# Key maxima behind a given step's minima, decode spread over steps 1 to 7, later attention loads on ScalarE's queue

## The chip, the core and the metric

The kernel runs on one core of one Trainium2 chip. The metric is device microseconds of one execution. Engines are TensorE (PE, with PEld its weight loads), VectorE (DVE), ScalarE (ACT), GpSimd (POOL) and SyncE (SP); "q" behind an engine's name is its instruction sequencer, which also issues DMAs.

## What is computed

Block-local attention over 2 batches, 8 heads, 768 positions and 64 channels, then two blocks of matrix products on its output.

```python
k_sum = k.reshape(B, H, nb, block, D).max(axis=3)      # nb = 24 blocks of 32 keys
v_sum = v.reshape(B, H, nb, block, D).mean(axis=3)
scores_l = scale * q @ k^T, only where |i - j| < 16
scores_s = scale * q @ k_sum^T + log(32)
a = softmax(concat([scores_l, scores_s]))
x = a @ concat([v, v_sum])                             # (2, 768, 512)
u = x + (relu(x^T @ w_tok1) @ w_tok2)^T ; x = u + relu(u @ w_ch1) @ w_ch2
out = x + relu(layernorm(x) * g @ moe2_w_ch1) @ moe2_w_ch2
```

## The kernel before

Attention works on 8 pairs of heads (i = 0 to 7), each in 3 steps, so there are 24 steps (n = 0 to 23, pair n // 3). A step covers four windows of 64 queries. Its parts are: `att_qk`, sixteen small score matmuls against 96 local keys and 24 block maxima; `att_exp`, on VectorE four fused instructions that scale, mask and take the minima of a window (the "minima"), and on ScalarE four exponentials; `att_tr`, transposes on TensorE; `att_evac`, ScalarE's copy out of PSUM; `att_av`, the product with the values; `att_norm`, VectorE's division; `att_hi` and `att_lo`, the split of the result for later products.

Before its first step each pair needs its loads (`load_pair`: keys, 480 KB, and queries, 384 KB; `load_v`: two value transfers of 306 KB; `load_vt`: transposed values, pairs 4 to 7), the maxima of its key blocks (`prep_k`, one VectorE reduction, and `copy_k` on ScalarE), and the sums of its value blocks: by summing matmuls for pairs 0 to 3 (`sum_v`, three parts of eight, and `write_sums` on ScalarE), on GpSimd for pairs 4 to 7 (`prep_v1`).

The scores of two successive steps lie in the same PSUM banks, so the scores of step n + 1 start only when the minima of step n are taken. The key, query and value buffers are three deep and are freed by pair i - 3.

The weights come as 62 "halves" of 128x512, at 64 bits an element. `load_half` loads one into one of three stage buffers. The conversion runs in ticks: a tick takes the magnitude of one half on ScalarE (L114), decodes the half before it by four VectorE instructions (L128, L130, L132, L136), casts an older one on ScalarE (L176), subtracts the cast on VectorE (L183), and issues the next load. A tick counts as four operations for `convert_all(n)` and `convert(n)`, the first tick as one. Only three slots for two halves each exist during attention, so only six halves are cast there; more can be decoded.

`attention` gives every part a due time in units of steps, from the table `ORDER` (L34), and writes the program in the order of due times (L613). TensorE keeps that order exactly. On the other engines and queues a scheduler orders the instructions by its own simulated readiness, with the written order as priority; each engine and queue then runs in order on the chip. Before step 8.58 two filler matmuls follow each step's scores (`fill`). From step 8.58 on the first products on attention's output are laid between the steps (`g1`, `g2`, `transpose_u`). In `before` the attribute `ops` sets how many conversion operations each `att_norm` carries along: none up to due time 3.5, then 3, then 2 from 8.58 on.

Of the kernel before, what the change touches and what calls it, by code (L numbers as in the profile page):

```python
# [14 lines left out]
ALU = mybir.AluOpType  # L15
AX = mybir.AxisListType
# [4 lines left out]
BLOCK, WINDOW = 32, 16  # L21
NB = S // BLOCK
# [4 lines left out]
NK = 96 + NB  # L27
# [4 lines left out]
LEAD = 3  # L32
NXN = 3
ORDER = {  # L34
    "load_k": -5.2, "load_vt": -5.1, "load_v": -4.7, "kmax": -1.3, "copy_k": -1.0, "vsum": -2.4,
    "vput": -0.2, "vsum0": 0.6, "vput0": 1.12, "exp": 0.5, "tr": 1.1, "evac": 1.55, "av": 2.15,
    "norm": 2.6, "hi": 2.65, "lo": 2.7, "conv": 3.5, "bg": 8.58, "fin": 0.97,
}
# [14 lines left out]
class Kern:  # L53
# [150 lines left out]
    def load_pair(self, i, queue=None):  # L204
        nc = self.nc
        queue = queue or nc.sync
        b, p = divmod(i, NPAIR)
        Q, K = self.Q[i % 3], self.K[i % 3]
        nc.sync.dma_start(K[:, 0:6, NB : NB + 160], self.k[b, p])
        queue.dma_start(Q, self.q[b, p])  # L210

    def load_vt(self, i):
        b, p = divmod(i, NPAIR)
        self.nc.sync.dma_start(self.VT[i % 2], self.vt[b, p])

    def load_v(self, i):
        nc = self.nc
        b, p = divmod(i, NPAIR)
        V = self.V[i % 3]
        nc.sync.dma_start(V[NB:NK, 0], self.v[b, p, 0])  # L220
        nc.sync.dma_start(V[0:96, 1], self.v[b, p, 1])

    def prep_k(self, i):
        nc = self.nc
        K = self.K[i % 3]
        ks = self.att.tile([P, NB], F32, tag="ks", bufs=2, name=f"ks{i}")
        nc.vector.tensor_reduce(
            ks.rearrange("p (v j) -> p v j", v=6),
            K[:, 0:6, NB + 16 : NB + 144].rearrange("p v (j k) -> p v j k", k=BLOCK),
            axis=AX.X,  # L230
            op=ALU.max,
        )
        self.ks[i] = ks

    def copy_k(self, i):
# [72 lines left out]
    def att_exp(self, n):  # L308
        nc = self.nc
        qd = n % 3  # L310
        ps = self.sc.pop(n)
        sn = self.att.tile([P, 4, NK], F32, tag="sn", bufs=2, name=f"sn{n}")
        mn = self.att.tile([P, 4], F32, tag="mn", bufs=3, name=f"mn{n}")
        pr = self.att.tile([P, 4, NK], F32, tag="pr", bufs=3, name=f"pr{n}")
        self.pr[n] = pr
        for u in range(4):
            w = 4 * qd + u
            mv = w % 2 if 0 < w < NW - 1 else 2 + w % 2
            nc.vector.tensor_tensor_reduce(  # L319
                sn[:, u],  # L320
                ps[:, u % 2, u // 2, :NK],
                self.mask[:, mv],
                scale=-SCALE,
                scalar=3e38,
                op0=ALU.add,
                op1=ALU.min,
                accum_out=mn[:, u : u + 1],
            )
            nc.scalar.activation(pr[:, u], sn[:, u], AF.Exp, bias=mn[:, u : u + 1], scale=-1.0)  # L329
# [233 lines left out]
    def attention(self):  # L563


        npair, nq = B * NPAIR, 3 * B * NPAIR
        O = ORDER
        ev = []
        put = lambda at, *fns: ev.append((at, len(ev), fns))
        for i in range(npair):  # L570
            at = 3 * i
            if i > 1:
                put(at + O["load_k"], lambda i=i: self.load_pair(i))
                if i >= NPAIR:
                    put(at + O["load_vt"], lambda i=i: self.load_vt(i))
                put(at + O["load_v"], lambda i=i: self.load_v(i))
            put(at + (O["kmax"] if i != 1 else -0.45), lambda i=i: self.prep_k(i))
            put(at + (O["copy_k"] if i != 1 else -0.44), lambda i=i: self.copy_k(i))
            if i < NPAIR:
                for part in range(3):  # L580
                    put((1.15 + 0.5 * part, at + part - 0.75, at + part - 0.75, 7.5 + 0.5 * part)[i], lambda i=i, part=part: self.sum_v(i, part))
                continue
            put(at + O["vsum"], lambda i=i: self.prep_v1(i))
            put(at + O["vput"], lambda i=i: self.prep_v2(i))
        for n in range(nq):
            put(n, lambda n=n: self.att_qk(n))
            if n < O["bg"]:
                put(n + 0.02, lambda: self.fill(2))
            put(n + O["exp"], lambda n=n: self.att_exp(n))
            put(n + O["tr"], lambda n=n: self.att_tr(n))  # L590
            put(n + O["evac"], lambda n=n: self.att_evac(n))
            put(n + O["av"], lambda n=n: self.att_av(n))
            put(n + O["norm"], lambda n=n: self.weave(self.att_norm(n), self.convert(self.ops)))
            put(n + O["hi"], lambda n=n: self.att_hi(n))
            put(n + O["lo"], lambda n=n: self.att_lo(n))
        put(0.0, lambda: self.load_half(0), lambda: self.load_half(1))
        put(O["conv"], lambda: setattr(self, "ops", 3))
        put(O["bg"], lambda: setattr(self, "ops", 2))
        x0, x1, w0, w1 = self.g1(0, 0), self.g1(0, 1), self.g1(1, 0), self.g1(1, 1)
        y, z0 = self.g2(0), self.transpose_u(0)  # L600
        pieces = [x0, x0, x1, x1, y, y, y, y, w0, w0, z0, z0, z0, y, z0, w1, w1, y]
        low = {x0: 5 + O["lo"], x1: 11 + O["lo"], w0: 17 + O["lo"], w1: 23 + O["lo"]}
        need = {x0: 3, x1: 3, w0: 3, y: 6}
        at = O["bg"]
        for k, g in enumerate(pieces):
            while at < low.get(g, 0):
                at += 1
            if g in need:
                put(at, lambda g=g: self.convert_until(need[g]))
            put(at, lambda g=g: self.begin(g))  # L610
            put(at + O["fin"], lambda g=g: self.end(g))
            at += 1
        for _, _, fns in sorted(ev, key=lambda e: e[:2]):  # L613
            for fn in fns:
                fn()
        while self.evacs:
            self.end(self.evacs[0])
# [21 lines left out]
    def run(self):  # L639
        tc, nc, ctx = self.tc, self.nc, self.ctx  # L640
# [11 lines left out]
        self.conv = self.conversion()  # L652
        self.evacs, self.ks, self.ready_xt = [], {}, set()
        self.xt, self.pr, self.pt, self.av, self.sc, self.pst = {}, {}, {}, {}, {}, {}
        self.acc, self.stats, self.xn = {}, {}, {}
        self.add_slots(slots_a, 3)

# [41 lines left out]
        for t in self.V:  # L699
            nc.scalar.dma_start(t[NK : NK + 1], self.guard)  # L700
        nc.sync.dma_start(self.gt, self.g)
        self.load_v(1)

        self.wps = self.ps_mm.tile([P, 512], F32, tag="mm", name="warm_ps")
        self.fill(15)
# [163 lines left out]
```

## Time and profile before

| | us |
|---|---|
| median of three runs | 611.26 (608.82 to 611.40) |
| the profiled execution's own time | 610.87 |
| its span, first to last instruction | 609.1 |
| TensorE busy | 589.4 |
| VectorE busy | 334.0 |
| ScalarE busy | 210.6 |
| mean granted TensorE clock | 0.986 |

Step 23's products with the values end near 107.3 us; what follows is matrix products on attention's output. The difference between the span and the execution's own time, 1.8 us, lies around the program. A share of busy time is a mean over the whole span; a stretch is read by its own rows.

### The profile page before, as it was taken

To read this page: it belongs to the slowest core of one execution; us is meant where nothing else is said; L and a number is where in the kernel's file an instruction comes from. 1 tells how busy PE (TensorE), PEld (TensorE's weight loads), DVE (VectorE), ACT (ScalarE), POOL (GpSimd) and SP (SyncE) were. 2 spreads that over 40 slices of the span, in tenths; PEclk is the share of its full clock that TensorE was granted. 3 is DMA by queue.
4 is the path that set the end of the run, shared out by engine and by line. 5 is a ranking of instruction groups with operands and counts; after the bars stand their busy time and mean duration, and the time that the engine had idled before them with its cause. 6 is when DMAs were issued, how large, how long until landed. Compare 5 with 4: busy or idle time off the path is not lost.

```text
span 609.1 us, 9241 instructions
## 1 busy us (share of the span) xinstructions
PE 589.4 (97%) x3661; PEld 517.0 (85%) x3661; DVE 334.0 (55%) x845; ACT 210.6 (35%) x450; POOL 35.2 (6%) x60
## 2 busy tenths in 40 slices
PE   5889899999999999999999999999999999999997
PEld 2768677879899889899888989999888989989996
DVE  2799765999368799788789951111153211111122
ACT  2697887544133344333444411110122111011110
POOL 2055312100000000000000000000000000000000
PEclk9798899999999999999999999999999999999999
DMA  9977810235224333233423200000000100000011
GB/s 269 317 243 244 255 58 4 70 108 179 93 70 139 103 104 107 101 108 135 135 74 104 70 1 1 0 1 1 0 30 23 53 1 0 1 1 0 1 52 53
DMA packets 21074, 50.40 MB, mean 83 GB/s; under 512 B 1955, under 2 KB 8483, under 8 KB 21030
## 3 DMA queue, kind: packets, MB, share of 16 engines
q1 hardware_dynamic: 20880, 49.39, 24.7%
q8 instruction: 29, 0.48, 0.3%
q10 hardware_dynamic: 150, 0.41, 0.2%
q14 instruction: 15, 0.12, 0.1%
HBM read 46.65 MB, written 3.15 MB: 82 GB/s over the span
## 4 chain that ended last, share of the span: by engine, by line
PE 88%; DMA 4%; ACT 3%; DVE 3%; issue 0%; SPq 0%; POOL 0%; DVEq 0%
PE g L199 2%; PE g L201 2%; PE g L200 2%; PE av L356 1%; ACT pr L329 1%; DMA stage<-in_wts_dram 1%; PE scores L299 1%; DMA V<-in_v_dram 1%; PE pt L336 1%; PE vsum L278 1%; PE tx L517 1%; DMA VT<-in_vt_dram 1%; DMA K<-in_k_dram 1%; ACT V L262 1%; PE tu L450 1%; PE acc_('x', 0)_0_3721 L200 1%
## 5 line engine op out<-in xcount | busy, mean ns | idle before, releaser
L114 ACT ACTIVATE dec<-stage 128x512 f32<-128x512 f32 x62 | 41.9, 675 | 8.1 <-DMA stage<-in_wts_dram 8.1
L136 DVE SCALAR_TENSOR_TENSOR dec<-stage,dec 128x512 uint32<-128x512 uint32 x62 | 43.6, 704 | 0.9
L132 DVE SCALAR_TENSOR_TENSOR dec<-stage,dec 128x512 uint32<-128x512 uint32 x62 | 43.3, 699 | 0.9
L176 ACT CAST wh<-dec 128x512 fp32r<-128x512 f32 x62 | 38.1, 616 | 13.6 <-DVE dec L136 13.4
L183 DVE TENSOR_TENSOR wl<-dec,wh 128x512 fp32r<-128x512 f32 x62 | 42.7, 690 | 0.0
L329 ACT ACTIVATE pr<-sn,mn 128x120 f32<-128x120 f32 x96 | 30.2, 384 | 8.9 <-DVE mn L319 8.8
L128 DVE TENSOR_SCALAR dec<-dec 128x512 f32<-128x512 f32 x62 | 27.1, 440 | 2.5 <-ACT dec L114 2.5
L130 DVE TENSOR_SCALAR dec<-dec 128x512 uint32<-128x512 uint32 x62 | 26.6, 429 | 0.9
L299 PE MATMUL scores<-K,Q 64*64 64x120 f32 x384 | 17.0, 298 | 7.8 <-DVE mn L319 7.2
L319 DVE CUSTOM_DVE_ANT_0 sn<-scores,mask 128x120 f32<-128x120 f32 x96 | 21.3, 277 | 2.5 <-PE scores L299 2.1
L396 POOL TENSOR_TENSOR xl<-u,xh 128x256 fp32r<-128x256 f32 x24 | 18.4, 766 | 66.7 <-ACT xh L387 62.4
L299 PEld LDWEIGHTS scores<-K,Q 64*64 64x64 f32 x384 | 11.1, 146 | 12.7 <-DVE mn L319 7.9
L356 PEld LDWEIGHTS av<-V,PT 121*64 121x64 f32 x384 | 14.2, 143 | 7.3 <-issue 3.6
L356 PE MATMUL av<-V,PT 121*64 121x65 f32 x384 | 17.8, 234 | 2.5 <-ACT V L262 1.9
L278 PE MATMUL vsum<-V,ind 120*120 120x128 f32 (+1 forms) x96 | 15.5, 318 | 1.8 <-ACT V L262 1.8
L336 PE MATMUL pt<-ident,pr 128*120 128x128 f32 x96 | 16.7, 299 | 0.0
L336 PEld LDWEIGHTS pt<-ident,pr 128*120 128x120 f32 x96 | 11.7, 147 | 4.9 <-issue 2.1
L278 PEld LDWEIGHTS vsum<-V,ind 120*120 120x120 f32 (+1 forms) x96 | 13.8, 218 | 2.4 <-ACT V L262 2.0
L199 PE MATMUL g<-xh,wh 128*128 128x256 f32 x48 | 14.1, 293 | 0.5 <-DVE u L433 0.5
L343 ACT COPY PT<-pt 120x512 f32<-120x512 f32 x24 | 13.8, 576 | 1.0 <-PE pt L336 0.8
L492 DVE TENSOR_SCALAR xn<-u,mv,rs 128x128 f32<-128x128 f32 x48 | 14.0, 340 | 0.0
L201 PE MATMUL g<-xh,wl 128*128 128x256 f32 x48 | 13.4, 278 | 0.0
(3003 smaller groups left out, 1695.7 us busy)
## 6 DMA issues: line engine op xcount, KB each, us to landing
stage<-in_wts_dram SPq DMA_DIRECT2D x62, 512.0 KB, 3.3
V<-in_v_dram SPq DMA_DIRECT2D x16, 306.0 KB, 5.0
K<-in_k_dram SPq DMA_DIRECT2D x8, 480.0 KB, 5.9
out_dram<-u SPq DMA_DIRECT2D x12, 256.0 KB, 2.1
Q<-in_q_dram SPq DMA_DIRECT2D x7, 384.0 KB, 5.8
VT<-in_vt_dram SPq DMA_DIRECT2D x4, 384.0 KB, 5.3
Q<-in_q_dram ACTq DMA_DIRECT2D x1, 384.0 KB, 3.1
mask<-in_mask_dram SPq DMA_DIRECT2D x1, 240.0 KB, 5.8
```

What stands on the lines that cost most here:

```text
L114: nc.scalar.activation(m, self.raw[n][:, :, 1].bitcast(F32), AF.Abs)
L128: nc.vector.tensor_scalar(m, m, MAG_LO, MAG_HI, op0=ALU.max, op1=ALU.min)
L130: nc.vector.tensor_scalar(mi, mi, 3, 0x3FFFFFF8, op0=ALU.logical_shift_left, op1=ALU.bitwise_and)
L132: nc.vector.scalar_tensor_tensor(mi, t[:, :, 1], 0xC0000000, mi, op0=ALU.bitwise_and, op1=ALU.bitwise_or)
L136: nc.vector.scalar_tensor_tensor(mi, t[:, :, 0], 29, mi, op0=ALU.logical_shift_right, op1=ALU.bitwise_or)
L176: self.nc.scalar.copy(self.slots[c if c < 16 else c - 16][0][:, s], x)
L183: self.nc.vector.tensor_tensor(wl[:, s], x, f32(wh[:, s]), op=ALU.subtract)
L278: self.nc.tensor.matmul(self.ps_sum[:NK, 0:P].rearrange("p (r c) -> p r c", r=2), self.ind[rows, j, NB - 4 * w : NB - 4 * w + NK], V[rows, ...
L299: nc.tensor.matmul(ps[cols, j, e, :NK], Q[rows, 64 * w : 64 * w + 64], K.rearrange("p v c -> p (v c)")[rows, a : a + NK], start=True, stop ...
L329: nc.scalar.activation(pr[:, u], sn[:, u], AF.Exp, bias=mn[:, u : u + 1], scale=-1.0)
L336: nc.tensor.transpose(ps[:NK, u * P : u * P + P], pr[:, u], self.ident)
L356: nc.tensor.matmul(ps[64 * j : 64 * j + 64, e, 65 * r : 65 * r + 65], pt[:, u * P + 64 * (r ^ j) : u * P + 64 * (r ^ j) + 64], V[:, j, 2 * ...
```

## The change

1. `prep_k`: from pair 1 on the key reduction gets an ordering edge behind the last of the minima of step 3i - 2. The edge is between instructions of VectorE alone.
2. Conversion: `ops` stays 0 until 8.58, and instead two operations are put at n + 0.55 and two at n + 0.8 for n = 1 to 7. The first two weight loads leave the due-time list and are issued in `run`, half 0 ahead of pair 1's values and half 1 behind them.
3. Loads: for pairs 2 to 7 keys, queries, transposed values and values are issued by ScalarE's queue. The values' due time goes from -4.7 to -3.9, relative to the pair's first step.

```diff
-    "load_k": -5.2, "load_vt": -5.1, "load_v": -4.7, ...
+    "load_k": -5.2, "load_vt": -5.1, "load_v": -3.9, ...
 def load_pair(self, i, queue=None):
-        nc.sync.dma_start(K[:, 0:6, NB : NB + 160], self.k[b, p])
+        (nc.sync if i < 2 else queue).dma_start(K[:, 0:6, NB : NB + 160], self.k[b, p])
         queue.dma_start(Q, self.q[b, p])
 def load_vt(self, i):
-        self.nc.sync.dma_start(self.VT[i % 2], self.vt[b, p])
+        (self.nc.sync if i < 2 else self.nc.scalar).dma_start(self.VT[i % 2], self.vt[b, p])
 def load_v(self, i):
-        nc.sync.dma_start(V[NB:NK, 0], self.v[b, p, 0])
-        nc.sync.dma_start(V[0:96, 1], self.v[b, p, 1])
+        queue = nc.sync if i < 2 else nc.scalar
+        queue.dma_start(V[NB:NK, 0], self.v[b, p, 0])
+        queue.dma_start(V[0:96, 1], self.v[b, p, 1])
 def prep_k(self, i):
-        nc.vector.tensor_reduce(ks..., op=ALU.max)
+        with self.tc.issue_after(self.ttr[3 * i - 2].ins) if i > 0 else ExitStack():
+            nc.vector.tensor_reduce(ks..., op=ALU.max)
 def att_exp(self, n):
-            nc.vector.tensor_tensor_reduce(
+            self.ttr[n] = nc.vector.tensor_tensor_reduce(
 def attention(self):
-                put(at + O["load_k"], lambda i=i: self.load_pair(i))
+                put(at + O["load_k"], lambda i=i: self.load_pair(i, self.nc.scalar))
-            put(at + (O["kmax"] if i != 1 else -0.45), lambda i=i: self.prep_k(i))
+            put(at + (O["kmax"] if i != 1 else -0.46), lambda i=i: self.prep_k(i))
             put(n + O["exp"], lambda n=n: self.att_exp(n))
+            if 1 <= n < 8:
+                put(n + 0.55, lambda: self.convert_all(2))
+                put(n + 0.8, lambda: self.convert_all(2))
-        put(0.0, lambda: self.load_half(0), lambda: self.load_half(1))
-        put(O["conv"], lambda: setattr(self, "ops", 3))
 def run(self):
         nc.sync.dma_start(self.gt, self.g)
+        self.load_half(0)
         self.load_v(1)
+        self.load_half(1)
```

## Rows read from the trace of the kernel before

**Rows 1.** Busy time by stretch: us, each engine's busy us (instructions), clock, DMA.
```profile
8.50:26.09 17.59, 10.32 (x93) 8.56 (x92) 10.06 (x38) 9.62 (x24) 0.00 (x0) 0.81 1.07 321
13.87:19.70 5.83, 5.83 (x38) 4.93 (x38) 2.69 (x12) 3.25 (x10) 0.00 (x0) 0.54 1.04 343
26.09:49.21 23.12, 21.27 (x248) 16.66 (x247) 20.99 (x75) 19.50 (x47) 11.55 (x18) 0.87 0.78 249
49.21:70.12 20.91, 18.77 (x265) 15.09 (x264) 18.78 (x77) 16.19 (x41) 10.17 (x15) 0.90 0.79 260
62.63:70.12 7.49, 7.20 (x110) 5.30 (x110) 6.22 (x34) 7.07 (x20) 2.34 (x5) 0.77 1.01 339
70.12:102.49 32.37, 32.29 (x430) 25.75 (x427) 18.83 (x102) 25.72 (x69) 7.42 (x12) 1.00 0.24 69
```

**Rows 2.** TensorE's timeline: start, us, what, [idle before, releaser].
```profile
7.33 0.64 PE L299 MATMUL scores<-K,Q 64*64 64x120 f32 x16 [0.57 <-ACT K L237]
...
13.87 1.07 PE L299 MATMUL scores<-K,Q 64*64 64x120 f32 x16 [5.37 <-DVE mn L319]
...
16.56 3.22 PE L278 MATMUL vsum<-V,ind 120*120 120x128 f32 x16
...
21.16 1.05 PE L278 MATMUL vsum<-V,ind 120*120 120x128 f32 x8
...
26.09 1.08 PE L299 MATMUL scores<-K,Q 64*64 64x120 f32 x16
...
49.21 0.98 PE L299 MATMUL scores<-K,Q 64*64 64x120 f32 x16
...
62.63 0.64 PE L299 MATMUL scores<-K,Q 64*64 64x120 f32 x16 [1.86 <-DVE mn L319]
```

**Rows 3.** VectorE's timeline, the same columns.
```profile
12.06 0.95 DVE L227 TENSOR_REDUCE ks<-K 128x24 f32<-128x768 f32 x1 [5.15 <-DMA K<-in_k_dram]
12.93 0.27 DVE L319 CUSTOM_DVE_ANT_0 sn<-scores,mask 128x120 f32<-128x120 f32 x1
...
21.26 0.27 DVE L319 CUSTOM_DVE_ANT_0 sn<-scores,mask 128x120 f32<-128x120 f32 x1
```

**Rows 4.** ScalarE's timeline, the same columns.
```profile
17.11 0.67 ACT L114 ACTIVATE dec<-stage 128x512 f32<-128x512 f32 x1 [2.58 <-DMA stage<-in_wts_dram]
```

**Rows 5.** The decode's tile up to 110 us: ns min/median/max, first and last start.
```profile
L114 ACT ACTIVATE dec<-stage x10: 650/674/693, 17.1 to 58.4; 128x512 f32<-128x512 f32 x10
L128 DVE TENSOR_SCALAR dec<-dec x10: 415/426/1236, 17.8 to 59.8; 128x512 f32<-128x512 f32 x10
L130 DVE TENSOR_SCALAR dec<-dec x10: 392/422/828, 18.3 to 62.6; 128x512 uint32<-128x512 uint32 x10
L132 DVE SCALAR_TENSOR_TENSOR dec<-stage,dec x10: 675/682/1441, 18.7 to 63.2; 128x512 uint32<-128x512 uint32 x10
L136 DVE SCALAR_TENSOR_TENSOR dec<-stage,dec x10: 660/692/1210, 19.5 to 65.2; 128x512 uint32<-128x512 uint32 x10
...
L183 DVE TENSOR_TENSOR wl<-dec,wh x7: 678/684/878, 22.4 to 109.7; 128x512 fp32r<-128x512 f32 x7
```

**Rows 6.** Stretch 26.09:49.21, line L136 alone: us, busy us (instructions).
```profile
26.09:49.21 23.12, 3.49 (x4) 0.87 0.78 249
```

**Rows 7.** SyncE's queue, 50 to 64 us: start, us that the issue took.
```profile
50.25 0.55 SPq L209 DMA_DIRECT2D K<-in_k_dram  x1
50.85 0.63 SPq L210 DMA_DIRECT2D Q<-in_q_dram  x1
...
53.24 0.38 SPq L214 DMA_DIRECT2D VT<-in_vt_dram  x1
...
61.93 0.38 SPq L220 DMA_DIRECT2D V<-in_v_dram  x1
```

**Rows 8.** SyncE's waits up to 110 us: total us, times, longest us.
```profile
SPq L166 <- DVE dec L136: 60.8, 10, 34.2
...
SPq L209 <- DMA K<-in_k_dram: 3.2, 2, 1.8
```

More of the change, by code (lines that the diff above doesn't have):

```diff
@@ L34 @@
 ORDER = {
-    "load_k": -5.2, "load_vt": -5.1, "load_v": -4.7, "kmax": -1.3, "copy_k": -1.0, "vsum": -2.4,
+    "load_k": -5.2, "load_vt": -5.1, "load_v": -3.9, "kmax": -1.3, "copy_k": -1.0, "vsum": -2.4,
     "vput": -0.2, "vsum0": 0.6, "vput0": 1.12, "exp": 0.5, "tr": 1.1, "evac": 1.55, "av": 2.15,
@@ L226, in prep_k @@
         ks = self.att.tile([P, NB], F32, tag="ks", bufs=2, name=f"ks{i}")
[L227 to L232, printed above, removed]
+        with self.tc.issue_after(self.ttr[3 * i - 2].ins) if i > 0 else ExitStack():
+            nc.vector.tensor_reduce(
+                ks.rearrange("p (v j) -> p v j", v=6),
+                K[:, 0:6, NB + 16 : NB + 144].rearrange("p v (j k) -> p v j k", k=BLOCK),
+                axis=AX.X,
+                op=ALU.max,
+            )
         self.ks[i] = ks
@@ L654, in run @@
         self.xt, self.pr, self.pt, self.av, self.sc, self.pst = {}, {}, {}, {}, {}, {}
+        self.ttr = {}
         self.acc, self.stats, self.xn = {}, {}, {}
```

## The prediction

> **What bounds the kernel now.** I read the table of stretches first [rows 1]. From 26.09 us on TensorE is nearly always busy: 21.27 of 23.12 us in steps 3 to 7, 32.29 of 32.37 us in 70.12:102.49. There a microsecond on another engine counts only if that engine has none to spare. The loose stretch is the start: from 8.50 to 26.09 TensorE works 10.32 of 17.59 us, at a granted clock of 0.81, and in 13.87:19.70 of that at 0.54, near the lower of the clock's two levels, 1.2 of 2.4 GHz. The change can win most there.
>
> TensorE's timeline [rows 2] says where. Step 0's scores start at 7.33; step 1's start only at 13.87, after 5.37 us idle, and the releaser named is the minima of step 0. VectorE's timeline [rows 3] shows that the minima did not wait for TensorE: VectorE stood 5.15 us until 12.06 for pair 1's keys to land, reduced them (0.95 us), and only then, at 12.93, began the minima of scores that had been ready since about 8.0. The order on VectorE, not data, cost these 5 us.
>
> Next is what ended the stretch after that. ScalarE stood 2.58 us for the first weight half, until 17.11 [rows 4]; VectorE decoded that half, took another key reduction, and reached step 2's minima at 21.26 [rows 3]. TensorE meanwhile ran sixteen summing matmuls in 3.22 us at 16.56, where eight take 1.05 us at 21.16 [rows 2]: the clock was low after the idle [rows 1]. Step 3 began at 26.09.
>
> In steps 3 to 7 three engines are close together: TensorE 21.27, VectorE 20.99, ScalarE 19.50 of 23.12 us [rows 1]. So what is added to VectorE or ScalarE here soon costs time. In 62.63:70.12 ScalarE is the fullest, 7.07 of 7.49 us. From 70.12 to 102.49 VectorE is busy only 18.83 us, so it has room there.
>
> **Part 1, key maxima held back.** One instruction per pair moves behind the minima of step 3i-2; nothing is added. Pair 1's reduction now follows step 1's minima. Step 0's minima can start at 8.0 instead of 12.93, and as step 1's scores followed 0.94 us behind them before (12.93 to 13.87) they start at 8.9: **4.9 us earlier** [rows 2, 3]. While VectorE waits for pair 1's keys (12.06, if they land as before) step 1's minima are past; behind that wait stand step 2's minima, due later, and the decode. What is late next? Two candidates. TensorE's own chain from step 1 to step 3 took 12.22 us; at the high clock it is about 2.4 us shorter: 1.1 us on the sixteen summing matmuls (3.22 against twice 1.05), and an estimated 1.3 us on the scores (1.07 against 0.64), the two fillers and the transposes. That would put step 3 at 18.8. The other candidate is the decode of half 0, whose instructions are now due at steps 1 and 2, ahead of step 2's minima in the program, and which in the trace already stands before them.
>
> **Part 2, decode spread over steps 1 to 7, first halves loaded earlier.** Work is moved, not added. Per half: 0.426 + 0.422 + 0.682 + 0.692 + 0.684 = 2.9 us on VectorE and 0.674 us and a cast of the same shape, together an estimated 1.3 us, on ScalarE [rows 5]. Its transfer is moved too: half 0 is now issued ahead of pair 1's values and half 1 behind them; before, both went behind them. Two value transfers of 306 KB (the arrays' sizes) are 1.9 us at the 321 GB/s of 8.50:26.09 [rows 1], so half 0 could land at 15.2 instead of 17.11. Against it, pair 2's four loads (480 + 384 + 612 KB, 4.6 us at the same rate) now leave by a second queue and may be served first: 19.8 at the other end. I take 17.1, the row itself, between the two. Then 0.67 us for the magnitude on ScalarE, 2.2 us for four decode steps, 0.9 us for step 2's minima and hand-over: step 3 at about 21.0 (18.9 and 23.7 at the ends). This is later than TensorE's chain, so it decides: **gain 5.1 us** against 26.09 (7.2 and 2.4 at the ends).
>
> Steps 3 to 7 then carry 20 decode operations by the program, five halves; the trace had the last decode operation four times in 26.09:49.21, as a window of that line alone shows [rows 6]. One half more on VectorE is 20.99 + 2.9 = 23.9 us for a stretch of 23.12 [rows 1]: about 0.8 us too much. In return VectorE is a half ahead from step 8 on; the idle of 1.86 us at 62.63, where TensorE waited for minima [rows 2], should then go, with perhaps 0.6 us of lower clock behind it (its scores' neighbours in 62.63:70.12 ran at 0.77 [rows 1]): **gain 2.5 us**, between 0 and 3.
>
> **Part 3, loads from pair 2 on by ScalarE's queue.** Issues took 0.55 (keys), 0.63 (queries), 0.38 (transposed values) and 0.38 us (values, two of them) on SyncE [rows 7]. Without the transposed values a pair is 1.94 us, with them 2.32: two pairs and four pairs, **13.2 us** of ScalarE's sequencer, at most; nothing, if the sequencer issues while the engine still works. No row shows such an issue between ScalarE's operations. By stretch: loads due in steps 3 to 7 (pair 3, and keys, queries, transposed values of pair 4) are 1.94 + 1.56 = 3.5 us, with the extra half's 1.3 us 4.8, where ScalarE idled 3.62 us [rows 1]: 1.2 us too much. As VectorE's 0.8 us too much lies in the same steps, I count **1.0 us lost** for both. In 62.63:70.12 ScalarE had 0.42 us left and gets about 2 us of issues: **1.5 us lost**. From 70.12 on 6.65 us are free for the remaining 3.1 us (0.76 + 1.56 + 0.76).
>
> What does the part bring? SyncE's queue was in order, and weight halves waited on it ten times, 60.8 us in all, for a decode to free their buffer [rows 8]; without the longest, 34.2 us, these are 26.6 us in which attention's loads stood behind them. The key load of pair 4, due 5.2 steps before step 12, left at 50.25 [rows 7], in step 8. The Trainium skill (DMA: Bandwidth & Descriptors, section Issuing engines are not separate DMA queues) says that issuing from several engines only saves the time on the sequencer; by that rule this load would not come earlier, and the sum would have 0 for it. The trace differs: what the shared queue cost was a wait for another load's buffer. Still, the idle at 62.63 ended on minima, not on a load [rows 2], and in 70.12:102.49 TensorE hardly idled at all [rows 1], so I take 0. More than the idle of steps 3 to 7, 23.12 - 21.27 = 1.9 us, is not to be had from earlier landings, and less than nothing only by the issues counted above.
>
> **Sum**, against the profiled execution's own 610.87 us: 5.1 - 1.0 + 2.5 - 1.5 = 5.1 us, **605.8 us**. After attention the program is unchanged, so I carry the shift to the end one for one. The median of the runs shown, 611.26, is 0.4 us above this execution, less than any term.
>
> **Rivals.**
> *All engines keep up.* Half 0 lands early (7.2 us), the issues on ScalarE hide, steps 3 to 7 run at TensorE's own 21.27 us (1.9), the later stall goes (2.5): 11.6 us, 599.3. For it: TensorE's work is the largest of the three in steps 3 to 7. Against: VectorE gets a half more there.
> *The wait only changes its name.* Half 0 at 19.8, step 3 at 23.7 (2.4 us), the late stall stays, 1.0 and 1.5 us are lost: 611.0, no change. For it: DMA was busy all the time from 8.50 to 26.09 (share 1.07 with overlaps), so a second queue speeds no byte. It holds if pair 2's loads are issued before half 0. The case in which VectorE's order is not changed by the edge is in it as well.
> *Slower: ScalarE becomes the bound.* Its queue is in order, and a load that waits holds exponentials, evacuations and value sums behind it, for which TensorE's transposes and products wait. All 13.2 us of issues on the path, against 5.1 and 2.5 us won: 616.5. SyncE's key loads also waited 3.2 us for an earlier key load to land [rows 8]; on ScalarE such a wait is a stall. It decides when ScalarE's free time is below what the loads need: 3.62, 4.7 (49.21:70.12 left 20.91 - 16.19) and 6.65 us are 15.0 us against 11.3 us from pair 3 on [rows 1, 7]. That fits on the whole, so this stays the smaller case.
>
> **Chances.** Forecast (602 to 608) 0.50; all keep up (below 602) 0.17; changed name (608 to 614) 0.18; slower (above 614) 0.15. The range 599 to 613 leaves out about half of the fast case and nearly all of the slow one, 0.2 together. Faster by over 0.5% (below 607.8; about what a measurement here can tell) is 0.64, within it 0.21, slower 0.15.
>
> **What would show it.** Right: no key reduction before step 0's minima, step 1's scores near 9, step 3's near 21, the load issues among ScalarE's operations, step 8 some 4 us before 49.21, no idle of 1.9 us near step 11. Wrong: ScalarE's longest waits ending with a landing, step 1 still after 12, or step 8 at or after 49; or a gain at step 8 that is gone when attention ends.

## The result and the profile after

The changed kernel takes **613.85 us** (median of 13 runs, 610.42 to 616.45), the kernel before 610.24 in 13 runs beside it: ratio 1.0059, interval 1.0038 to 1.0081. It is slower by 0.6%. The forecast was 605.8 with a range of 599 to 613, so the time lies outside the range and on the other side of the kernel before. The profiled execution took 613.28 us (span 611.5) against 610.87 (span 609.1).

Start of a step's scores on TensorE, in us, each from a timeline; column +/- is what the change lost (+) or won (-) in the stretch that ends there:

| step | before | after | +/- |
|---|---|---|---|
| 1 | 13.87 | 8.64 | |
| 3 | 26.09 | 24.35 | -1.74 |
| 8 | 49.21 | 47.80 | +0.33 |
| 9 | 54.90 | 55.27 | +1.78 |
| 11 | 62.63 | 61.07 | -1.93 |
| 14 | 70.12 | 69.39 | +0.83 |
| 15 | 74.42 | 76.22 | +2.53 |
| 23 | 102.49 | 105.14 | +0.85 |

The same stretches from the table of stretches of the changed kernel (columns as in [rows 1]):

```profile
6.97:24.35 17.38, 11.68 (x111) 8.82 (x111) 9.26 (x37) 8.89 (x22) 0.00 (x0) 0.87 1.06 314
24.35:47.80 23.45, 19.62 (x247) 15.20 (x247) 21.68 (x76) 18.58 (x45) 3.78 (x5) 0.94 0.70 220
47.80:55.27 7.47, 6.85 (x66) 5.38 (x65) 4.17 (x15) 4.80 (x12) 3.80 (x8) 0.82 1.00 291
61.07:69.39 8.32, 6.38 (x114) 4.41 (x110) 6.23 (x33) 7.70 (x21) 4.29 (x9) 1.00 0.40 112
69.39:76.22 6.83, 4.82 (x59) 3.75 (x56) 2.12 (x12) 4.09 (x13) 2.98 (x5) 1.00 0.79 251
```

**The start.** TensorE's timeline after the change, which answers to [rows 2]:

```profile
6.97 0.64 PE L301 MATMUL scores<-K,Q 64*64 64x120 f32 x16
8.64 0.62 PE L301 MATMUL scores<-K,Q 64*64 64x120 f32 x13 [0.48 <-DVE mn L321]
...
12.55 1.33 PE L338 MATMUL pt<-ident,pr 128*120 128x128 f32 x4 [2.74 <-ACT pr L331]
13.67 3.21 PE L280 MATMUL vsum<-V,ind 120*120 120x128 f32 x16
16.81 0.64 PE L301 MATMUL scores<-K,Q 64*64 64x120 f32 x16
...
21.19 0.33 PE L358 MATMUL av<-V,PT 121*64 121x65 f32 x2 [1.88 <-ACT V L264]
...
24.35 1.07 PE L301 MATMUL scores<-K,Q 64*64 64x120 f32 x16
```

Step 1's scores start at 8.64, as forecast (8.9): the idle of 5.37 us [rows 2] is 0.48. But the next line shown waits 2.74 us for step 0's exponentials, and the products that stand ahead of step 3 wait 1.88 us for value sums, both from ScalarE. Its timeline (ACTq is its queue of DMA issues), then the first of step 2's minima on VectorE:

```profile
9.10 0.63 ACTq L209 DMA_DIRECT2D K<-in_k_dram  x1
11.70 0.36 ACTq L210 DMA_DIRECT2D Q<-in_q_dram  x1
12.11 1.25 ACT L331 ACTIVATE pr<-sn,mn 128x120 f32<-128x120 f32 x4 [5.18 <-DMA K<-in_k_dram]
14.93 0.66 ACT L114 ACTIVATE dec<-stage 128x512 f32<-128x512 f32 x1 [1.57 <-DMA stage<-in_wts_dram]
...
18.92 0.66 ACT L114 ACTIVATE dec<-stage 128x512 f32<-128x512 f32 x1 [1.72 <-DMA stage<-in_wts_dram]
...
20.35 1.62 ACT L264 ACTIVATE V<-vsum 24x768 f32<-24x768 f32 x2
```

```profile
18.61 0.28 DVE L321 CUSTOM_DVE_ANT_0 sn<-scores,mask 128x120 f32<-128x120 f32 x1
```

The minima of step 0 began at 7.68 on VectorE, so the exponentials could start soon after. ScalarE stood idle for 5.18 us before them, behind pair 2's query load, which left only at 11.70, when pair 1's key load had landed (both loads use the same semaphore in the trace): where VectorE had waited for pair 1's keys [rows 3], ScalarE now did. Half 0 came early (magnitude at 14.93, not 17.11 [rows 4]). Half 1's magnitude, at 18.92, stands ahead of the exponentials and value sums that step 3 needs, but it can have cost little: the first of step 2's minima began at 18.61, and the summing matmuls that the value sums need ended near 19.3.

**Steps 8 to 9 and 14 to 15.** GpSimd's timeline, which the prediction did not read, then TensorE's behind it:

```profile
50.76 2.50 POOL L249 TENSOR_TENSOR VT<-VT 128x384 f32<-128x384 f32 x4 [8.07 <-DMA VT<-in_vt_dram]
...
53.71 0.72 POOL L398 TENSOR_TENSOR xl<-u,xh 128x256 fp32r<-128x256 f32 x1
...
73.59 1.00 POOL L249 TENSOR_TENSOR VT<-VT 128x384 f32<-128x384 f32 x1 [3.77 <-DMA VT<-in_vt_dram]
74.55 0.72 POOL L398 TENSOR_TENSOR xl<-u,xh 128x256 fp32r<-128x256 f32 x1
```

```profile
54.48 0.38 PE L200 MATMUL g<-xl,wh 128*128 128x256 f32 x1 [0.62 <-POOL xl L398]
...
75.33 0.39 PE L200 MATMUL g<-xl,wh 128*128 128x256 f32 x1 [1.86 <-POOL xl L398]
```

GpSimd sums the transposed values (VT) and forms the low parts xl of the attention's output, in one order. It now waits for VT, and TensorE's first products wait for the xl behind it. In the list of waits up to 110 us, before and after:

```profile
POOL VT L247 <- DMA VT<-in_vt_dram: 4.7, 3, 2.6
```

```profile
POOL VT L249 <- DMA VT<-in_vt_dram: 18.0, 4, 8.1
```

VT lands late because it is issued late. First and last of the four loads on SyncE before, then on ScalarE after:

```profile
24.86 0.42 SPq L214 DMA_DIRECT2D VT<-in_vt_dram  x1
...
53.24 0.38 SPq L214 DMA_DIRECT2D VT<-in_vt_dram  x1
```

```profile
43.28 0.45 ACTq L214 DMA_DIRECT2D VT<-in_vt_dram  x1
...
80.12 0.39 ACTq L214 DMA_DIRECT2D VT<-in_vt_dram  x1
```

The due place in the program is the same (5.1 steps ahead). On SyncE only other issues and their waits stand before it; on ScalarE also the work of the engine that the scheduler put ahead of it. It is this order that sets when VT leaves, not the queue alone: in e7 below, with VT on ScalarE's queue as well, the first two VT issues were put ahead of nearly all of that work.

```profile
8.89 1.24 ACTq L214 DMA_DIRECT2D VT<-in_vt_dram  x2
```

**Steps 15 to 23.** Here the 0.85 us lie in step 16 alone (3.36 us before, 4.21 after). TensorE waits there for hh, a result that ScalarE writes, not for GpSimd:

```profile
83.34 0.50 PE L199 MATMUL g<-hh,wh 128*128 128x512 f32 x1 [0.35 <-ACT hh L417]
```

Step 16 takes the same 4.21 us in e6 and e8 below, which have VT back on SyncE, and 3.36 us in e1, e2 and e4, which have no part 3.

### The profile page after: what moved, and what is told of

Its sections match the earlier page's. It is cut to its first block, busy times and chain, and to the rows that moved or that the text cites. A ratio compares the mean times of both kernels' runs of the same rounds, so it can differ in the third digit from the quotient of the medians.

```text
span 611.5 us, 9239 instructions
## 1 busy us (share of the span) xinstructions
PE 589.7 (96%) x3661; PEld 515.1 (84%) x3661; DVE 333.1 (54%) x845; ACT 210.7 (34%) x450; POOL 31.8 (5%) x60
## 4 chain that ended last, share of the span: by engine, by line
PE 88%; DMA 4%; ACT 4%; DVE 2%; POOL 1%; issue 1%; ACTq 0%; DVEq 0%
DMA VT<-in_vt_dram 2%; PE g L199 2%; DMA K<-in_k_dram 2%; PE g L200 2%; PE g L201 2%; ACT pr L331 2%; PE vsum L280 1%; PE av L358 1%; PE scores L301 1%; PE pt L338 1%; PE tx L519 1%; PE tu L452 1%; PE acc_('x', 2)_0_4722 L200 1%; PE acc_('x', 0)_0_3721 L200 1%; PE acc_('x', 0)_2_3723 L200 1%
## 5 line engine op out<-in xcount | busy, mean ns | idle before, releaser
L136 DVE SCALAR_TENSOR_TENSOR dec<-stage,dec 128x512 uint32<-128x512 uint32 x62 | 42.5, 686 | 1.0
L280 PEld LDWEIGHTS vsum<-V,ind 120*120 120x120 f32 (+1 forms) x96 | 13.2, 210 | 3.7 <-ACT V L264 3.2
L200 PE MATMUL g<-xl,wh 128*128 128x256 f32 x48 | 13.6, 284 | 2.5 <-POOL xl L398 2.5
```

Of the source, the lines that this page charges most:

```text
L136: nc.vector.scalar_tensor_tensor(mi, t[:, :, 0], 29, mi, op0=ALU.logical_shift_right, op1=ALU.bitwise_or)
L200: nc.tensor.matmul(out, lhs[0], rhs[1], start=False, stop=False)
L280: self.nc.tensor.matmul(self.ps_sum[:NK, 0:P].rearrange("p (r c) -> p r c", r=2), self.ind[rows, j, NB - 4 * w : NB - 4 * w + NK], V[rows, ...
```

## Experiments

All start times of steps come from the timelines of the profiled executions.

| run | step 3 | step 7 | step 8 | step 9 | ratio to before (95%) |
|---|---|---|---|---|---|
| before | 26.09 | 40.91 | 49.21 | 54.90 | 1 |
| changed kernel | 24.35 | 39.22 | 47.80 | 55.27 | 1.0059 (1.0038, 1.0081) |
| e1 | 27.45 | 41.30 | 48.63 | 53.98 | 1.0036 (1.0022, 1.0050) |
| e2 | 26.61 | 40.07 | 49.10 | 55.74 | 1.0007 (0.9992, 1.0022) |
| e3 | 30.51 | 43.98 | 51.02 | 57.15 | 1.0215 (1.0154, 1.0276) |
| e4 | 26.16 | 39.50 | 47.47 | 54.07 | 1.0038 (1.0022, 1.0054) |
| e5 | 18.62 | 38.70 | 49.74 | 55.38 | 1.0028 (1.0011, 1.0045) |
| e6 | 23.46 | 43.22 | 50.45 | 55.80 | 1.0080 (1.0053, 1.0106) |
| e7 | 26.94 | 40.49 | 51.01 | 56.86 | 1.0057 (1.0035, 1.0079) |
| e8 | 25.55 | 39.59 | 52.10 | 57.98 | 1.0060 (1.0038, 1.0081) |
| e9 | 19.59 | 33.37 | 48.45 | 54.86 | 0.9998 (0.9983, 1.0013) |
| e10 | 27.91 | 42.57 | 52.72 | 59.04 | 1.0041 (1.0020, 1.0062) |
| e11 | 23.41 | 37.27 | 46.44 | 52.46 | 1.0096 (1.0065, 1.0127) |
| e12 | 18.16 | 33.46 | 41.77 | 51.70 | 0.9943 (0.9927, 0.9959) |
| e13 | 27.92 | 42.44 | 51.68 | 58.32 | 1.0040 (1.0020, 1.0060) |
| e14 | 29.06 | 44.31 | 52.91 | 58.30 | 1.0115 (1.0090, 1.0141) |
| e15 | 26.34 | 41.30 | 50.65 | 55.94 | 1.0042 (1.0025, 1.0060) |
| e16 | 18.32 | 32.70 | 48.49 | 54.83 | 1.0030 (1.0012, 1.0048) |
| e17 | 25.83 | 39.56 | 46.59 | 51.95 | 0.9996 (0.9980, 1.0012) |
| e18 | 19.64 | 33.44 | 46.72 | 52.62 | 0.9949 (0.9925, 0.9973) |

**The parts one by one.** e1 is part 1 (the hunks of `prep_k` and `kmax`), e2 part 2 (`load_half`, `convert_all`), e3 part 3 (`load_k`, `load_vt`, `load_v`), e4 parts 1 and 2.

```
e1, e4:  + with self.tc.issue_after(self.ttr[3 * i - 2].ins) if i > 0 ...
e2, e4:  + put(n + 0.55, lambda: self.convert_all(2)) ...
e3:      + (self.nc.sync if i < 2 else self.nc.scalar).dma_start(self.VT ...
```

> The kernel before with part 1 alone (key maxima behind the minima of step 3i-2). Theory (part 3 is what cost the time, part 1 pays): step 1's scores start near 8.9 instead of 13.87, step 3's near 21 to 23 instead of 26.09, and the time is 3 to 5 us under the kernel before, about 606. Rival A (the wait only changes its name: the first weight half, landing at 17, ends the next wait whatever VectorE did before it): step 1's scores early, step 3's after 25, the time within 2 us of before.

> The kernel before with part 2 alone (decode at steps 1 to 7, half 0's load ahead of pair 1's values). Theory: within 2 us of before, since only where the decode stands changes. Rival B (the decode in the tight steps 3 to 7 is what cost the time): 2 us or more slower than before, and steps 3 to 8 take more than 24.5 us where they took 23.1.

> The kernel before with part 3 alone (attention's loads from pair 2 on by ScalarE's queue, values due at -3.9). Theory: 2 to 5 us slower than before, 612 to 616: a wait of ScalarE ends on a landing in the first 20 us, and GpSimd's splits of attention's output (xl) stand behind sums that wait for transposed values, so that the first products start later. Rival B: within 2 us of before.

> Parts 1 and 2 without part 3: the changed kernel with all of attention's loads back on SyncE's queue. Theory: step 3's scores near 20 to 22, step 8's 3 to 5 us before 49.2, time 604 to 608. Rival A: step 3's after 24 and within 2 us of before, 609 to 612. Rival B: as slow as the changed kernel or slower, 612 and more.

Part 1 alone is slower by 0.36%, though step 2's scores started at 13.02 (before 19.71): the theory's 3 to 5 us of gain did not come, and step 3 is where rival A had it. ScalarE and TensorE of e1:

```profile
17.11 0.66 ACT L114 ACTIVATE dec<-stage 128x512 f32<-128x512 f32 x1 [6.78 <-DMA stage<-in_wts_dram]
17.68 1.24 ACT L330 ACTIVATE pr<-sn,mn 128x120 f32<-128x120 f32 x4
```

```profile
18.11 1.32 PE L337 MATMUL pt<-ident,pr 128*120 128x128 f32 x4 [3.91 <-ACT pr L330]
...
23.50 0.48 PE L357 MATMUL av<-V,PT 121*64 121x65 f32 x2 [2.37 <-ACT V L263]
...
58.88 0.64 PE L300 MATMUL scores<-K,Q 64*64 64x120 f32 x16 [0.79 <-DVE mn L320]
...
63.29 1.08 PE L300 MATMUL scores<-K,Q 64*64 64x120 f32 x16 [2.57 <-DVE mn L320]
```

Half 0 lands at the same time as before, and step 1's exponentials stand behind its magnitude. What was won at 8 us is lost at 17. At step 9 e1 is still 0.9 us ahead of the kernel before, at step 13 it is 1.9 us behind (69.80 against 67.87), and the waits for minima lie between: 0.79 and 2.57 us, where the kernel before had 1.86 [rows 2]. VectorE has the decode ahead of these minima. The instructions on the decode's tile alone, from step 9's scores to step 11's (us, VectorE's busy us, ScalarE's, clock, DMA), in the kernel before, the changed one, e1 and e4:

```profile
54.90:62.63 7.73, 4.08 (x6) 0.65 (x1) 1.00 0.53 189
```

```profile
55.27:61.07 5.80, 0.00 (x0) 0.00 (x0) 1.00 0.54 170
```

```profile
53.98:63.29 9.31, 6.41 (x10) 1.36 (x2) 0.97 0.67 220
```

```profile
54.07:63.00 8.93, 6.25 (x8) 0.68 (x1) 1.00 0.71 252
```

The more decode falls here, the longer these two steps take. Of these versions only the changed kernel has none left here. Parts 1 and 2 without part 3 (e4) have more than the kernel before, and so has part 2 alone (5.01 us of it in 7.80).

Part 2 alone changes nothing that these runs resolve, and adds nothing to part 1; e4 came out as rival A said, not 604 to 608. Part 3 alone costs 2.15%, far more than the 2 to 5 us expected. Its profile is 4.4 us behind at step 3, GpSimd waits 18.6 us for VT, and step 14 takes 8.37 us where it took 4.30. Of the changed kernel's 0.59% only some 0.2 are left for part 3 beside e4's 0.38 (their intervals overlap), so its price depends on the other parts.

**Is it ScalarE's order at the start?** e5 is e1 with one more edge: the magnitude of half 0 behind step 2's exponentials.

```
+ with self.tc.issue_after(self.ex[2].ins) if n == 0 else ExitStack():
      nc.scalar.activation(m, self.raw[n][:, :, 1].bitcast(F32), AF.Abs)
```

> Part 1 alone, and an ordering edge on ScalarE: the magnitude of half 0 (the first instruction of the decode) stands behind the exponentials of step 2. Theory (after part 1 the start is held by ScalarE's order: the wait for half 0's landing near 17 stands ahead of the exponentials of step 1): that wait of 6.8 us is gone from between the exponentials, TensorE's idle before step 0's transposes or step 1's too, step 3's scores start at 18 to 21 instead of 27.45, and the time is 605 to 608. Rival (the decode that starts later is what the next steps wait for, so it is given back): step 3's scores early, step 9's not before 53, and the time within 1 us of part 1 alone, 611 to 613.

Step 3 starts at 18.62, 7.5 us before [rows 2]: in part 1 alone this wait did set it. But step 5 starts at 31.21, for the wait has moved to half 2, and the time, 611.29 us, is the rival's:

```profile
25.39 0.66 ACT L115 ACTIVATE dec<-stage 128x512 f32<-128x512 f32 x1 [6.25 <-DMA stage<-in_wts_dram]
```

**Is the loss of the changed kernel its queue?** e6 gives the VT loads back to SyncE, e7 all loads of pair 2, e8 both.

```
e6: - (self.nc.sync if i < 2 else self.nc.scalar).dma_start(self.VT ...
e6: + self.nc.sync.dma_start(self.VT ...
e7: - queue = nc.sync if i < 2 else nc.scalar
e7: + queue = nc.sync if i < 3 else nc.scalar
```

> The changed kernel, but transposed values by SyncE's queue as before. Theory (late transposed values hold GpSimd, whose splits xl stand behind the sums, and the first products wait for xl): GpSimd's waits of 8.1 and 3.8 us for a landing are gone, step 9 starts near 53.5 instead of 55.27 and step 15 near 72 instead of 76.22, the time is 3 to 4 us under the changed kernel, about 610. Rival (ScalarE's issues and the start are what costs): within 1 us of the changed kernel.

> The changed kernel, but pair 2's four loads by SyncE's queue as before; from pair 3 on by ScalarE's. Theory: ScalarE no longer stands 5.2 us until 12.11 for a landing that frees a DMA's semaphore, but the next wait, for half 0 at 14.9, takes most of its place: step 3 gains 0 to 2 us on 24.35, the time 0 to 2 us under the changed kernel. Rival (the issues at the start are the main cost): step 3 before 21 and the time 3 us or more under the changed kernel.

> Both of these together: keys, queries and values from pair 3 on by ScalarE's queue, all else as in the changed kernel. Theory: the sum of the two, 4 to 5 us under the changed kernel, 608 to 610, not slower than the kernel before. Rival (ScalarE's remaining issues cost by themselves): still above 612.

None is shown to be faster than the changed kernel, so the theories' totals of e6 and e8 were missed. e6 removes the stall at step 15 (74.77 in its profile, 76.22 in the changed kernel), but steps 8 and 9 come later, and its median, 614.09, is no lower. In e6 and e8 nothing on TensorE waits over 0.3 us directly for GpSimd any more during attention. So the VT wait is where this profile loses time, but it is not shown that the change would gain without it.

Nor does taking away the wait behind pair 2's query load bring step 3 forward. In e7 and e8 that load is off ScalarE's queue, and step 3 comes later than in the changed kernel, not earlier (26.94 and 25.55 against 24.35). The next wait takes its place: step 0's exponentials now stand behind half 0's magnitude (14.84 in e7, 13.97 in e8; in e4, which has no part 3, 14.70). TensorE of e7:

```profile
15.84 1.32 PE L338 MATMUL pt<-ident,pr 128*120 128x128 f32 x4 [6.28 <-ACT pr L331]
```

**All magnitudes behind exponentials, with and without landings.** e9 is e1 with every magnitude behind the last exponential emitted; e10, e11 and e12 are the kernel before, the changed one and e9 without the loads of halves 3 to 12.

```
e9:   + with self.tc.issue_after(self.ex[max(self.ex)].ins) if self.ex and n < 13 ...
e10 to e12:
      + if self.wide and 3 <= h < 13:
      +     t = self.old[h % 3]
```

> Part 1 alone, and every magnitude that ScalarE takes of a weight half in the attention is issued behind the last exponential that the program had emitted by then (half 0 and 1 behind that of step 3, half 2 behind that of step 4), so that no exponential of the early steps stands behind a landing weight half. Theory (ScalarE waits in order for landings, and what stands behind them paces TensorE): step 3's scores at 18 to 20 us as in the run with one magnitude held, step 5's at 25 to 28 and not 31.2; most of the early gain is then still there at step 9 (49 to 53 us, before: 54.9), and the total is 605 to 609.5 us. Rival (the landings themselves pace the stretch; whatever is freed at one place waits at the next): step 9 at 54 to 56 us again, total 610 to 613 us.

> The kernel before, but the loads of weight halves 3 to 12 in the attention are left out: their decode reads the tiles of halves 0 to 2 again (all instructions of the engines stay, the weights are wrong). Some 5.2 MB of the transfers of the first 70 us are gone. Theory (landings pace the first 55 us): step 3 stays at 25 to 26 us (it waits for half 0), but step 9 starts at 47 to 51 us instead of 54.9, and the total is 602 to 607 us. Rival (the engines' own work paces steps 3 to 9, the waits for halves only fill its gaps): step 9 at 53.5 us or later, total 609 us or more.

> The changed kernel with the loads of weight halves 3 to 12 left out in the same way (the decode reads the tiles of halves 0 to 2 again; the weights are wrong). Theory (the change's early start is eaten by landings of halves, and its late VT loads cost beside): step 9 at 45 to 50 us; with the queues freer, VT lands some us sooner, step 15 at 66 to 71 us, and the total is 600 to 606 us, level with the kernel before without these loads or up to 3 us under it. Rival (the cost of the change is the waits of ScalarE's issues and not the landings of weights): 3 us or more above the kernel before without these loads.

> Part 1 with all magnitudes behind exponentials, and the loads of weight halves 3 to 12 left out (the decode reads the tiles of halves 0 to 2 again; the weights are wrong). Theory (landings and the order on ScalarE pace the start): step 3 at 18 to 20 us, step 9 at 42 to 47 us, total 597 to 603 us. Rival (the engines' own work paces): step 9 at 50 us or later, total 606 us or more.

e9 is level with the kernel before (610.38 against 610.36 us): part 1's loss is gone, and steps 3 and 5 (26.24) are where the theory had them. Step 7 starts 7.5 us sooner, but step 8 only 0.8, so step 9 and the total went as the rival said. ScalarE and TensorE of e9 show the place:

```profile
40.60 0.66 ACT L115 ACTIVATE dec<-stage 128x512 f32<-128x512 f32 x1 [6.33 <-DMA stage<-in_wts_dram]
...
43.09 1.61 ACT L264 ACTIVATE V<-vsum 24x768 f32<-24x768 f32 x2
```

```profile
44.75 3.77 PE L280 MATMUL vsum<-V,ind 120*120 120x128 f32 x16 [8.07 <-ACT V L264]
```

The value sums that stand ahead of step 8 wait until ScalarE has written those of the pair before, and ScalarE stands at a landing half. e10 came out as the rival said: without the loads the kernel before is slower by 0.4%, with step 9 at 59.04. VectorE is nearly full, in e10's table of stretches for steps 3 to 7:

```profile
27.91:52.72 24.81, 20.93 (x244) 16.97 (x246) 23.65 (x76) 21.10 (x49) 17.20 (x26) 0.84 0.46 133
```

e11 is at 616.0 us, 2.8 above e10, near the rival's 3, though step 9 lay at 52.46; TensorE waited 3.99 us for xl at 74.26. So the change loses about as much without those landings as with them (2.8 and 3.6 us; e11 ran from 613.81 to 619.43). e12 is the first that is faster than the kernel before, 606.78 us, but it too came out as its rival said: step 9 is at 51.70 where the theory had 42 to 47, and the total is above the theory's 597 to 603. Against e9, the same edges with the loads, it is 3.6 us less: that is what these loads cost there. Its step 8 is at 41.77, and then GpSimd holds TensorE (TensorE's timeline):

```profile
48.21 0.46 PE L205 MATMUL g<-xl,wh 128*128 128x256 f32 x1 [2.32 <-POOL xl L402]
```

**Is it VectorE's decode, due by step 9?** e13 and e14 leave out three of VectorE's four passes for halves 0 to 5, e15 and e16 give their low parts to GpSimd.

```
e13, e14:  + if h < 6: ... return    (behind the clamp, yields kept)
e15, e16:  + eng = self.nc.gpsimd if h < 6 else self.nc.vector
```

> The kernel before, with VectorE's decode of weight halves 0 to 5 cut: of its four passes only the clamp stays, the shift and the two bit merges are left out (0.48 + 0.69 + 0.82 us a half, 12 us in all; the weights of these halves are wrong). Loads, ScalarE's magnitudes and casts and the subtractions stay. Theory (VectorE's attention work and the decode that is due by step 9 fill VectorE from step 3 to 9 and set step 9): step 9 starts 5 us or more sooner than 54.9 (44 to 50 us), and the total is 602 to 607 us. Rival (landings of halves, or ScalarE's own work, set step 9): step 9 at 53 us or later, total 608.5 to 611 us.

> The changed kernel with the same passes of halves 0 to 5 left out (the weights of these halves are wrong). Theory (VectorE's due work ate the start's gain): step 9 at 44 to 50 us, and at or before that of the kernel before with the same cut; what the change still loses is GpSimd's wait for VT behind it (2 to 4 us at step 15), so the total is 603 to 609 us. Rival (the change's own waits on ScalarE set step 9): step 9 at 53.5 us or later, total 611 us or more, as without the cut.

> The kernel before, with the six subtractions that give the low parts of weight halves 0 to 5 (0.72 us each on VectorE, 4.3 us in all) done by GpSimd instead; everything is computed. Theory (VectorE's work sets step 9): step 9 2 to 4 us sooner (51 to 53 us), total 607 to 609.5 us, unless GpSimd's pass takes much longer than its 0.73 us for half as many columns (1.5 us expected) and holds its VT and xl work. Rival (something other than VectorE): step 9 at 54.5 us or later, total 610 to 612 us.

> Part 1 with every magnitude behind exponentials, and the six subtractions of halves 0 to 5 on GpSimd; everything is computed. Theory (VectorE's work sets step 9, and here ScalarE's wait of some 6 us for a landing half near 40 us too): step 9 at 51 to 54 us (54.9 with the subtractions on VectorE), total 606 to 609.5 us. Rival: step 9 at 54.5 us or later, total 610 us or more.

No. In e13 VectorE is busy 17.68 of the 23.76 us of steps 3 to 7, where it was 20.99 of 23.12 [rows 1], and they take no less:

```profile
27.92:51.68 23.76, 20.79 (x244) 16.89 (x246) 17.68 (x66) 18.87 (x45) 10.03 (x15) 0.86 0.81 259
```

e14 (617.5 us), e15 and e16 have their step 9 where their rivals had it too. The totals of e13 (612.16 us) and e15 (612.79) even lie above their rivals' 611 and 612, and why less work on VectorE makes the kernel slower is not shown. GpSimd took 1.30 us for a subtraction, and in e15 and e16 TensorE never waits over 0.3 us for it, so the move itself does not hide a gain. A full VectorE is not what steps 3 to 7 hang on; from step 9 to 11 it is another matter, as e1 showed.

**No early decode at all.** e17 is the kernel before, e18 is e1, both without any decode of halves 0 to 5 (loads kept, a constant tile in their place).

```
+ if 6 <= n < NHALF:     (magnitude; passes, casts and subtractions likewise)
```

> The kernel before, with the decode of weight halves 0 to 5 left out on ScalarE and VectorE (magnitudes, four passes, casts and subtractions; their loads stay; one constant tile stands for these weights, so they are wrong). Theory (the decode on both engines, with ScalarE's waits for landing halves, is what stretches steps 2 to 9): step 3 at 22 to 24 us, since step 1's wait for the key maxima stays, and step 9 at 41 to 47 us instead of 54.9; total 597 to 605 us. Rival (the attention's own chain of scores, exponentials and value sums paces these steps): step 9 at 52 us or later, total 607 us or more.

> Part 1 alone, with the decode of halves 0 to 5 left out in the same way. Theory (the decode absorbed the start's gain): step 3 at 18 to 20 us, and step 9 at least 3 us ahead of the same cut in the kernel before (38 to 43 us), total 2.5 to 5 us under it. Rival (the attention's own chain, or the landings of pairs 2 and 3, absorbs it): step 9 within 1 us of the same cut in the kernel before, and the totals within 1 us of each other.

e17 ended near its rival's end (step 9 at 51.95, 610.64 us): of the 23.12 us of steps 3 to 7 the early decode accounts for 2.4, the rest stays without it, and the total does not change. e18 takes 607.05 us, 3.6 less, as the theory had the difference; but step 9 is within 0.7 us, as the rival had it, and the spans of the two profiles differ by 0.6 us only (e17's profiled run, at 609.0, is among its lower ones). Where the 3.6 us come from is therefore open. In e18 step 7 is 6.1 us ahead of e17, step 8 no more: half 6, the first that is decoded, stands ahead of the value sums. TensorE of e17, then ScalarE and TensorE of e18:

```profile
44.65 2.02 PE L291 MATMUL vsum<-V,ind 120*120 120x128 f32 x16 [1.78 <-ACT V L275]
```

```profile
40.80 0.66 ACT L114 ACTIVATE dec<-stage 128x512 f32<-128x512 f32 x1 [4.26 <-DMA stage<-in_wts_dram]
41.36 1.61 ACT L276 ACTIVATE V<-vsum 24x768 f32<-24x768 f32 x2
...
43.03 3.77 PE L292 MATMUL vsum<-V,ind 120*120 120x128 f32 x16 [6.29 <-ACT V L276]
```

It is e9's mechanism again, with 4.26 us of landing and 1.75 us of low clock (3.77 against 2.02 for the same sixteen matmuls; the granted clock was 0.50 in 43.03:46.72 of e18 and 1.00 in 44.65:46.60 of e17).

## Why the prediction was wrong

**First failing step: what decides step 3.** The prediction let step 3 follow step 2's minima, by two chains, TensorE's and the decode of half 0 on VectorE. The decode's chain held: from half 0's magnitude to step 2's minima it took 3.68 us (14.93 to 18.61), where 0.67 + 2.2 and a key reduction of 0.95 make 3.8. The step that failed is the last term, 0.9 us for step 2's minima and the hand-over to step 3. From the first of step 2's minima to step 3's scores the changed kernel takes 5.74 us (18.61 to 24.35), and the rows of before had said 4.83 (21.26 to 26.09 [rows 2, 3]). In between, step 3 waits for TensorE's products of the steps before, and these for exponentials and value sums of ScalarE. ScalarE's queue was read for one row [rows 4] and not for what stood behind that row. e1 and e5 show it: the same early minima of steps 0 and 1, step 3 at 27.45 with half 0's magnitude ahead of step 1's exponentials and 18.62 with it behind. That 18.62 is close to the 18.8 that the prediction had for TensorE's own chain. The term of 5.1 us was 1.74, although half 0 came early: by the prediction's sum a magnitude at 14.93 would have given more than 7 us.

**Second: part 3's own wait at the start.** That a waiting issue stalls ScalarE stood in the rival, but at no place; the first one stood ahead of step 0's exponentials, and ScalarE idled 5.18 us. The rival *the wait only changes its name* is what happened here, by an issue and not by half 0, which came early. Without that issue it is half 0 after all, and step 3 is later still (e7, e8). So two waits stood side by side, and no run takes both off the changed kernel.

**Third: GpSimd was left out.** Part 3 moves four VT loads, and their only reader is GpSimd, which works in order with xl behind VT. The prediction priced the issues and took 0 for landings, with no loss beyond the issues as the bound; that bound was wrong. Stretches 8 to 9, 14 to 15 and 15 to 23 lost 1.78 + 2.53 + 0.85 = 5.2 us, where the sum had nothing. The rows tie 0.62 and 1.86 us of this to xl directly. The 0.85 lie in step 16 and are not VT's, since e6 and e8 have them too. How the rest divides (the clock was 0.82 in the first stretch) is open, and so is what the VT wait costs in the end, since e6 and e8, without it, are no faster.

**The terms that held, one of them by luck.** Steps 3 to 7 lost 0.33 where 1.0 was said, with five last decode operations there as counted against four [rows 6]. The idle of 1.86 us at step 11 went, and steps 9 to 11 won 1.93 where 2.5 was said, with no decode left there. But the prediction booked both on part 2, and part 2 does not do it: e4 has four last decode operations in steps 3 to 7, and steps 9 to 11 take 7.80 us in e2 and 8.93 in e4, against 7.73 before. Only with part 3 added do steps 9 to 11 win (5.80 in the changed kernel), and for what part 3 brings the prediction had taken 0. Steps 11 to 14 lost 0.83 where 1.5 was said. The rival that charged all 13.2 us of issues was far off: only 1.94 us of ScalarE's idle from 24 to 83 us ends on an issue, behind a key, a query and a VT load at 41.39 to 43.73. TensorE waited for the value sums behind it before step 8, 2.99 us where the kernel before had 1.78:

```profile
45.51 2.36 PE L280 MATMUL vsum<-V,ind 120*120 120x128 f32 x16 [2.99 <-ACT V L264]
```

```profile
45.99 3.28 PE L278 MATMUL vsum<-V,ind 120*120 120x128 f32 x16 [1.78 <-ACT V L262]
```

The Trainium skill's rule (DMA: Bandwidth & Descriptors, section Issuing engines are not separate DMA queues), cited there, agrees with the trace in that no transfer time was gained: the DMA share of the start is 1.06 after and 1.07 before [rows 1].

The four terms of the sum came to 1.74 - 0.33 + 1.93 - 0.83 = 2.5 us instead of 5.1, and 5.2 us that the sum did not have went the other way: 2.7 us slower at step 23, 2.4 in the span. The medians say 3.6.

**Where a start's gain goes.** With part 1 and the magnitudes held or left out, 6.4 to 7.8 us are won at step 3 (e5, e9, e16, e18). At step 8 no more than 0.8 are left in e5, e9 and e16, and in e18 2.5 against the kernel before, but nothing against e17, which has as little decode. The place is shown in e9 and e18: step 8's value sums wait for ScalarE, and ScalarE for a landing half. Neither VectorE's decode (e13, e15) nor later landings alone (e10) explains steps 3 to 9 of the kernel before. Taken together, the order and no later landings (e12) won 3.5 us.

Part 1 alone (e1) loses its time from step 9 to 13, where VectorE's decode stands ahead of the minima; that is read from traces, and no run tests it by itself. Open are why the kernel before gets slower without these loads or with less decode, and what the changed kernel would take without both of its waits at the start. No version with all its work done beat the kernel before.

## What to carry to other kernels

When a wait is taken off one in-order engine, list what the waiting consumers still need from every other in-order engine, with what stands ahead of it there, a landing above all: a gain is real up to the next such place. Check the hand-over that a sum assumes against the same hand-over in the old trace: here 0.9 us was assumed where the rows had 4.83. Before a load is moved to a compute engine's queue, look at who reads it, and when its issue will be reached behind that engine's work.

## What the runs showed of the hardware

A waiting issue on ScalarE's queue kept ScalarE idle for 5.18 us ahead of its exponentials, though its own duration is 0.36 us: it left at 11.70, when pair 1's key load had landed, and they began at 12.11. The other issues mostly ran beside ScalarE's work: 24 issues from 24 to 110 us are 12.1 us of issuing, and 2.2 us of idle ended on them (1.94 and 0.29).

TensorE's clock made some idle time dearer: the same sixteen summing matmuls took 2.02 us behind 1.78 us of idle in e17 (granted clock 1.00), 3.77 us behind 6.29 in e18 and 3.77 behind 8.07 in e9 (0.50 in both, the lower level). The length of the idle just before them does not decide it by itself: they took 3.28 us behind the same 1.78 in the kernel before (0.59), 3.77 behind 2.24 in e13 (0.50), and 2.36 behind 2.99 in the changed kernel (0.83).
